# First FFN layer: a PSUM bank filled whole before it is read, 512 columns per read, and a new order of all operations

## Chip, cores and metric

The kernel runs on one core of one Trainium2 chip. The metric is the device time of one execution in microseconds (us). The figure for a kernel is the median of its runs.

## What is computed

Windowed attention, a real-part 2-D Fourier transform, a normalization and a two-layer feed-forward network (FFN), all in fp32. The shapes are q, k, v of (8, 8, 576, 64), which give 4608 tokens of 512 values, and two FFN weights of 512x2048 and 2048x512.

```python
scores = np.where(mask, scale * q @ k.T, -1e9)      # window of 64 positions
attn = softmax(scores) @ v                          # 8 heads of 64
x = attn.transpose(0, 2, 1, 3).reshape(B, S, 512)
u = x + np.real(np.fft.fft(np.fft.fft(x, axis=1), axis=2))
un = (u - mean(u)) / np.sqrt(var(u) + 1e-6)
out = u + np.maximum(un @ w_ch1, 0.0) @ w_ch2
```

## The kernel before

**Tiling.** The 4608 tokens are 36 tiles of 128 tokens. `attn_tile` does the attention of one tile, `fft` the transform of one batch entry, `norm_tile` the sum with the transform and the normalization. Two tiles make a chunk of 256 tokens (`CH`), and there are 18 chunks. fp32 accuracy is reached by splitting every operand into two fp16 parts and multiplying three of the four combinations (`PASSES`), so each logical product is three matmuls. Only the first tiles and the first chunk (chunk 0, the "plain" one) run in true fp32. Chunks 0 to 12 use `ffn(c)`, which the change rewrites; chunks 13 to 17 use `ffn7(c)`, a form of the second layer with seven products instead of eight, whose code the change leaves alone.

**The FFN step.** `ffn(c)` runs over f = 0..15, blocks of 128 of the 2048 hidden values. The first layer of block f (L1405) writes 128x256 fp32, that is half of a PSUM bank: blocks 2p and 2p+1 are the two halves of one bank `ph` (tag `f1`, two banks in all). I call them the first and the second half of pair p. Each half is 12 matmuls of 256 columns. The result is read twice: ScalarE (ACT) applies the ReLU and stores the high fp16 part `hh` (L1420), then VectorE (DVE) stores the low part, max(ph, 0) minus the high part (L1423). I call these two the eviction of a half. They are issued for every half by itself, 256 columns each; there are four `hh` buffers. The second layer of block f (L1386) then takes `hh` as stationary operand: 6 matmuls of 512 columns into the two banks `po`. When all 16 blocks are in, DVE adds `po` to the residual `xu` (L1443) and SyncE stores it.

**Order of the work.** Nothing is left to a scheduler at run time. Every operation is handed to a planner, `Plan.op`, with an engine, an assumed duration, a priority, and the buffers that it reads, writes and holds. `Plan.order` walks the engines in model time and emits all operations in one global order, which becomes each engine's program order. FFN matmuls have priorities from 1e6 up, so TensorE (PE) uses them as filler between attention and transform work; evictions have priority -10, ahead of nearly everything on ACT and DVE. The tables `NUDGE`, `LEAD` and `BIAS` shift priorities and engine choices of single operations. They are numbers found by a search, one set per kernel. Some elementwise operations may go to DVE or to GpSimd (POOL), as the planner finds (`alt`). While the program has not reached the FFN, planned gaps of PE are filled with dummy matmuls (`warm`, L1685). Waits between engines are put in by the framework from the tiles that the emitted operations touch.

Three things in the code matter for what follows. `holds=[bpair]` keeps a bank until both its halves are evicted. In `op("PE", ..., bank1, ..., [bph] if f % 2 else [bph, bfirst], holds=[bpair])` a second half is ordered after the first half and after nothing else. The eviction of the first half may stand in the emitted order ahead of the second half's matmuls or behind them.

```python
"xe": 1, "r3": 3, "fh": 5, "g": 2, "mp": 2, "mt": 1, "un": 2, "up": 1, "big": 4, "hh": 4,
op("PE", 1.73 if plain else 1.31, 1e6 + 32 * c + 2 * f, bank1, [Bu[c], *bws, bfirst], [bph] if f % 2 else [bph, bfirst], holds=[bpair])
op("ACT", 0.28, -10, lambda g=h_part: g(0), [bph], [bh], holds=[bpair])
```

Of the kernel before, what the change touches and what calls it, by code (L numbers as in the profile page):

```python
# [63 lines left out]
    "": {0: 3.6, 1: -0.1, 2: 2.4, 3: -4.7, 4: 0.6, 5: -15.8, 6: -1.7, 7: 0.7, 8: -10.1, 10: 8.4, 11: 17.7},  # L64
    "even": {0: -15.1, 1: 6.7, 2: 27, 3: 18, 4: -20.7, 5: -8.2, 6: -2, 7: 10.7, 8: -16.2, 9: 30.8, 10: -1.9, 11: -5.8, 12: 14.5, 13: -1.2, 14: -0.8, 15: -18.3, 16: 12.5, 18: -0.9, 19: -14.6, 20: -0.5, 22: 7.1, 23: 16.8, 24: -24.7, 25: -1, 26: 19, 27: -1.4, 28: 3.9, 29: -7.5, 30: 1.6, 31: 7.5, 32: -1.3, 34: -9.3, 35: 0.6, 36: -77.6, 37: 16, 38: -6.9, 39: -15.3, 40: -26, 41: 2.8, 43: 10.1, 44: 5},
    "ffn7": {0: 13, 1: -5.4, 2: 0.7, 3: 0.8, 4: 12.9, 5: -11.4, 6: 4.6, 8: 5.2, 9: -4, 10: 0.2, 11: -11.1, 13: -21.7, 14: 2.4, 15: 13, 16: -8.2, 17: 2.1, 18: 6.5, 19: -6.9, 21: 31.5, 22: -9.4, 23: -1.3, 24: 9.8, 25: -3.1, 26: -2.1, 27: 18.5, 28: 34.5, 29: 14.4, 30: 5.9, 31: -10.6, 32: -2.3, 33: 0.3, 34: 5.7, 35: 3, 37: 7.4, 38: 2, 39: 20.6, 40: -4.3, 41: 9.3, 43: -1.2, 44: 1.1, 45: -1.1, 46: 3.9, 47: 19, 48: 0.9, 50: 1.1, 51: 1.4, 52: -1.8, 53: 2.3, 54: -0.5, 55: -26.2, 57: -1.4, 58: 0.2, 59: -23.3, 60: -6.3, 61: -1.3, 62: 3.3, 63: 14.3, 64: -1.6, 65: 7.3, 66: 9.5, 67: 7, 68: 0.6, 69: 4.5, 70: -15.4, 71: -4.1, 72: 2.5, 73: 20.1, 74: 4.1, 75: -9.1, 76: 6.7},
    "first": {0: 9.1, 2: -4.8, 3: -2.3, 4: -2.5, 5: -3.9, 6: 48.2, 7: -4.8, 8: -7.6, 9: -1.3, 12: -12, 13: -1.6, 14: -2.4, 15: 0.4, 16: -1.4, 17: -6.8, 18: -6.5, 19: 3.5, 20: -20.5, 21: -14.9, 22: -5.2, 23: 35.3, 24: 23.3, 25: -13.8, 26: -30.6, 27: 44.4, 28: 0.9, 29: -6.7, 30: 1.2, 32: -0.8, 33: 18, 34: 12, 35: 11.7, 60: -4.6, 61: -1.3, 62: 16.6, 63: -3.1, 70: -19},
    "norm": {0: 9.7, 1: 4.6, 2: -5.6, 3: -5.3, 4: 22.8, 5: -8.4, 6: 0.7, 8: -0.2, 10: 4.1},
    "odd": {0: -6.1, 1: 8.3, 2: -10.5, 3: -0.9, 4: -0.1, 5: 0.4, 6: -10, 7: 12.3, 8: 1, 9: -21.6, 10: 11.6, 11: 11.4, 12: 0.2, 13: 0.5, 14: 0.5, 15: -5.7, 17: -7.6, 18: 2.3, 19: 2.1, 20: 7.5, 21: -3.7, 22: 0.5, 23: -8.9, 24: 1, 25: -1.2, 26: -0.3, 27: 6, 28: 0.8, 29: 8.5, 31: 12.9, 32: -4, 33: -5.6, 35: 8.9, 36: 17.5, 37: 6.6, 38: 4.2, 39: -6.6},
    "part": {1: -2},  # L70
    "piece": {0: 28.4, 2: -6.6, 3: 7, 4: -0.6},
    "prep": {0: -4.8, 1: -0.4, 2: 3.9, 4: 14.6, 5: -3.5, 6: -28.8, 7: 4.1, 8: 6.4, 10: 1.8, 11: -2.4},
    "scale": {0: -15.1, 2: -2.4, 3: -0.8, 4: 5.4},
    "split": {0: -7.5, 1: 4.1, 2: 1, 3: 0.9, 4: -0.5, 6: 24.5, 7: 5.8, 8: -1.2, 9: 3, 10: 32.6, 11: -1.8, 12: -24, 13: 3.6, 14: 0.9, 15: -7.4, 16: -0.2, 17: -1.2, 18: 1.3, 19: 0.8, 20: 2, 22: -22, 23: 14.6, 24: 29.2, 25: 2, 26: -12.3, 28: -29.8, 29: 3.4, 30: -18.6, 31: 16, 32: 2.1, 33: -31.6, 50: 0.3, 51: -2, 53: -20.8, 54: 1.5, 55: -1.9, 56: 7.8, 57: -15.2},
    "tail": {0: -8.3, 1: 3.4, 2: 0.2, 10: 28.5, 11: -0.7, 12: -0.7},
    "whole": {0: 4, 1: 4.2, 2: 3.1, 3: 9.3, 4: -3, 5: 27.2, 6: 15.9, 7: -2.2, 8: 8.6, 9: 14.4, 10: -1.8, 12: 50.7, 13: 4, 14: 15.5, 15: 6.6, 16: 0.5, 17: 2, 18: -0.1, 19: 6.3, 20: 1.7, 21: -1.3, 22: -1.3, 23: -8.4, 50: -16.8, 51: -5.1, 55: 29.8, 56: 1.4, 57: -6.4},
# [124 lines left out]
class Plan:  # L201
# [6 lines left out]
    PATIENT = {"DVE": 0, "ACT": 0.25, "POOL": 0.25, "DMA": 0}  # L208
# [169 lines left out]
def attn_fft_ffn_kernel(ctx: ExitStack, tc: tile.TileContext, q, k, v, w1, w2, gidx, dft_d, dft_s, mask, out):  # L378
# [11 lines left out]
        "xe": 1, "r3": 3, "fh": 5, "g": 2, "mp": 2, "mt": 1, "un": 2, "up": 1, "big": 4, "hh": 4,  # L390
# [978 lines left out]
    def ffn(c):  # L1369
# [7 lines left out]
        def second(f, bh):  # L1377
            def go():
                if f == 0:
                    t["po"] = [bank("f2", f"po{c}_{i}", (P, DM)) for i in range(2)]  # L1380
                hh = t["hh", f]
                for i in range(2):
                    sl = slice(P * i, P * i + P)
                    mm = [(hh[:, sl], wf[1][f])] if plain else [(hh[:, a, sl], wp[1][:, f, b_]) for a, b_ in PASSES]
                    for x, (l_, r_) in enumerate(mm):
                        nc.tensor.matmul(  # L1386
                            t["po"][i], l_, r_, start=(f == 0 and x == 0), stop=(f == NKF - 1 and x == len(mm) - 1)
                        )
# [328 lines left out]
```

## Time and profile before

| | before |
|---|---|
| three runs | 988.84, 991.28, 986.29 us; median 988.84 us |
| profiled execution | 987.79 us, of which the span of the trace is 986.0 us |
| PE, matmuls | 959.6 us busy, 97% of the span, 9362 matmuls |
| DVE | 748.6 us, 76% |
| ACT | 463.4 us, 47% |
| POOL | 186.3 us, 19% |
| granted PE clock, mean | 0.995 of 2.4 GHz |

Each engine is a queue that runs in its program order. An engine's busy time counts instructions, and its idle time counts the gaps before them; a gap's "releaser" is what ended the wait. Matmuls overlap one another, so a group's busy time is the union of their spans, while "mean ns" is the length of one from issue to landing. In a timeline the step from one group's start to the next group's start is the cost on PE.

### The profile page before, as it was taken

Reading aid. Unit: us, or ns where it says so; the run is one execution under the profiler, and the core shown is the slowest. Engines: PE = TensorE matmul, PEld = TensorE weight load, DVE = VectorE, ACT = ScalarE, POOL = GpSimd, SP = SyncE. Lnnn points to the kernel's source line nnn. Section 1 sums busy time; section 2 is a strip of 40 time slices with the busy share of each in tenths; the row PEclk is TensorE's granted clock in tenths of the full one; section 3 lists DMA queues with packets and bytes.
Section 4 is the critical chain, followed back from the end, with each engine's and each line's share of the span. In section 5 each row is a group of like instructions: output and inputs, shape, how many; then the busy total and the mean of one; then the engine's idle time right before and its main releaser. Section 6 shows DMA issues by size and latency. Waiting matters only on the chain.

```text
span 986.0 us, 23773 instructions
## 1 busy us (share of the span) xinstructions
PE 959.6 (97%) x9362; PEld 718.1 (73%) x9362; DVE 748.6 (76%) x1926; ACT 463.4 (47%) x1218; POOL 186.3 (19%) x196
## 2 busy tenths in 40 slices
PE   8999999999999999999999999999989999999997
PEld 6867677666676677666776676667666788888886
DVE  4878988878876887768777786788887986676436
ACT  5756687643553444545553553456322243333312
POOL 2111012122332222312213322221113101100000
PEclk9999999999999999999999999999999999999999
DMA  9988884238999768797858479975423312221000
GB/s 196 272 231 246 244 172 85 86 75 194 159 214 182 172 127 204 151 189 160 185 142 197 109 186 195 185 159 137 87 59 79 60 54 63 66 65 33 1 23 22
DMA packets 316704, 134.76 MB, mean 137 GB/s; under 512 B 293032, under 2 KB 293160, under 8 KB 316592
## 3 DMA queue, kind: packets, MB, share of 16 engines
q1 hardware_dynamic: 313872, 124.33, 56.1%
q0 software_dynamic: 2720, 8.92, 3.6%
q8 instruction: 73, 1.20, 0.5%
q14 instruction: 39, 0.32, 0.1%
HBM read 62.85 MB, written 22.04 MB: 86 GB/s over the span
## 4 chain that ended last, share of the span: by engine, by line
PE 78%; DVE 11%; DMA 5%; SPq 2%; ACT 2%; issue 1%; POOL 0%; DVEq 0%; ACTq 0%; POOLq 0%
PE ph L1405 23%; PE po L1386 20%; PE ph L1527 11%; PE q L1582 9%; PE pa L778 3%; PE pz L1101 2%; PE pg L1049 2%; PE psc L666 2%; DVE hh L1423 2%; DVE y L825 1%; DMA pt<-flex 1%; PE psc L680 1%; DMA kst<-flex 1%; PE pp L724 1%; SPq L744 1%
## 5 line engine op out<-in xcount | busy, mean ns | idle before, releaser
L1405 PE MATMUL ph<-uhl,w0s 128*128 128x256 f16 (+1 forms) x2424 | 311.6, 279 | 10.8 <-DVE hh L1423 9.6
L1386 PE MATMUL po<-w1s,hh 128*128 128x512 f16 (+1 forms) x1216 | 310.8, 391 | 0.0
L1405 PEld LDWEIGHTS <-w0s 128*128 128x128 f16 x2304 | 224.9, 98 | 74.4 <-issue 15.1
L1420 ACT ACTIVATE hh<-ph 128x256 f16<-128x256 f32 x192 | 73.9, 385 | 239.7 <-PE ph L1405 199.7
L1386 PEld LDWEIGHTS <-hh 128*128 128x128 f16 x1152 | 109.8, 98 | 96.2
L1423 DVE SCALAR_TENSOR_TENSOR hh<-ph,hh 128x256 f16<-128x256 f32 x192 | 80.6, 421 | 86.5 <-ACT hh L1420 60.6
L1527 PE MATMUL ph<-uhl,w0s 128*128 128x256 f16 x960 | 108.6, 273 | 0.0
L1527 PEld LDWEIGHTS <-w0s 128*128 128x128 f16 x960 | 93.9, 98 | 11.5
L1210 POOL TENSOR_TENSOR rs<-mv,mhalf 128x1 f32<-128x1 f32 x36 | 22.0, 610 | 279.9 <-DVE mv L1206 278.7
L1546 ACT ACTIVATE flex<-ph 128x512 f32<-128x512 f32 x40 | 23.9, 599 | 98.0 <-PE ph L1527 97.9
L1551 DVE TENSOR_TENSOR flex<-flex 128x256 f32<-128x256 f32 x80 | 34.6, 432 | 35.9 <-ACT flex L1546 34.1
L709 ACT ACTIVATE pr<-pr,nm 128x128 f32<-128x128 f32 x184 | 58.3, 394 | 3.5 <-DVE nm L700 3.5
L1582 PEld LDWEIGHTS <-qbd 128*128 128x128 f16 x480 | 47.0, 98 | 5.4
L738 POOL TENSOR_TENSOR flex<-pr,flex 128x512 f16<-128x512 f32 x24 | 29.4, 1227 | 96.0 <-ACT flex L485 47.0
L1186 POOL DMA_INDIRECT mt<-md,gix x34 | 36.6, 1077 | 45.9 <-DMA md<-mp 36.9
L793 ACT ACTIVATE xa<-pa,rc 128x64 f32<-128x64 f32 x184 | 41.5, 324 | 7.7 <-DVE rc L786 3.6
L700 DVE CUSTOM_DVE_ANT_0 pr<-psc,mskb 128x128 f32<-128x128 f32 x184 | 41.3, 285 | 4.1 <-PE psc L666 3.9
L1582 PEld LDWEIGHTS <-kst 128*128 128x128 f16 x360 | 35.2, 98 | 4.1
L778 PE MATMUL pa<-v,pt 128*64 128x65 f16 (+1 forms) x1328 | 31.0, 201 | 1.2 <-DMA pt<-flex 1.2
L576 POOL TENSOR_TENSOR flex<-qn,flex 128x1024 f16<-128x1024 f32 x11 | 23.7, 2153 | 43.3 <-ACT flex L485 26.2
L825 DVE TENSOR_TENSOR y<-xa 128x256 f32<-128x256 f32 x60 | 29.2, 528 | 0.9 <-ACT xa L793 0.7
L1582 PE MATMUL q<-w1s,qbd 128*128 128x256 f16 x240 | 29.5, 273 | 0.0
(219 smaller groups left out, 1520.6 us busy)
## 6 DMA issues: line engine op xcount, KB each, us to landing
wd<-in_moe_w_ch SPq DMA_DIRECT2D x26, 512.0 KB
out<-xu SPq DMA_DIRECT2D x36, 256.0 KB
kn<-in_k SPq DMA_DIRECT2D x32, 256.0 KB
qn<-in_q SPq DMA_DIRECT2D x32, 256.0 KB
xd<-xa SPq DMA_DIRECT2D x30, 256.0 KB
xu<-xd SPq DMA_DIRECT2D x30, 256.0 KB
flex<-in_v SPq DMA_DIRECT2D x20, 256.0 KB
v<-v SPq DMA_DIRECT2D x36, 130.0 KB
```

Of the source, the lines that this page charges most:

```text
L700: nc.vector.tensor_tensor_reduce(out=t["pr", jj][:, hp], in0=t["ps", jj][:, hp], in1=mskb[:, m : m + P], scale=-0.125, scalar=3.0e38, op0= ...
L709: nc.scalar.activation(pr, src, AF.Exp, bias=t["nm", jj][:, hp : hp + 1], scale=-1.0)
L778: nc.tensor.matmul(pa[half_, hh], pt, v_, start=(x == 0), stop=(x == len(mm) - 1))
L793: nc.scalar.mul(xv[:, hh], pa[:, hh, 0:64], rc[:, hh])
L825: eng.tensor_tensor(out=o, in0=p0, in1=p1, op=al)
L1186: nc.gpsimd.indirect_dma_start(out=mts[T], out_offset=None, in_=mds[pb][0 : HR if n < 4 else 2 * HR], in_offset=bass.IndirectOffsetOnAxis( ...
L1386: nc.tensor.matmul(t["po"][i], l_, r_, start=(f == 0 and x == 0), stop=(f == NKF - 1 and x == len(mm) - 1))
L1405: nc.tensor.matmul(ph, l_, r_, start=(x == 0), stop=(x == len(mm) - 1))
L1420: nc.scalar.activation(t["hh", f][:, 0], ph, AF.Relu)
L1423: nc.vector.scalar_tensor_tensor(out=hh[:, 1], in0=ph, scalar=0.0, in1=hh[:, 0], op0=ALU.max, op1=ALU.subtract)
L1527: nc.tensor.matmul(ph, l_, r_, start=(x == 0), stop=(x == len(mm) - 1))
L1582: nc.tensor.matmul(t["q"][q_][:, y], l_[:, a, i, m], r_(b_, m), start=(s_ + y + m + x == 0), stop=(s_ == 3 and m == 1 and x == 2 and (y == ...
```

## The change

The two halves of a pair are computed into their bank as before, and only then is the bank read: one ACT instruction and one DVE instruction of 512 columns per pair, in place of two and two of 256. `hh` becomes one tile for both blocks of a pair, with two buffers in place of four (the same bytes). The bank belongs to the pair as a whole, so `holds` is gone. The second layer's priorities go by pairs. `PATIENT["POOL"]` goes from 0.25 to 1 (how far the planner lets POOL wait for an operation of better priority). All three tables are searched anew: `NUDGE` (17 lines), `LEAD` and `BIAS`, of which one line stands here. Line numbers behind L1405 shift by one or two. In the built order, ahead of the first FFN matmul there stand 55 dummy matmuls and the scores of nine tiles (before: 46 and eight). `u_lo` (L1233) goes from 24 on DVE and 10 on POOL to 31 and 3, `k_lo` (L565) from 10 and 13 to 15 and 8. The matmuls that do real work are the same ones, as many as before.

```diff
-    "part": {1: -2},
+    "part": {0: 1.1, 1: -5.2},
...
-    PATIENT = {"DVE": 0, "ACT": 0.25, "POOL": 0.25, "DMA": 0}
+    PATIENT = {"DVE": 0, "ACT": 0.25, "POOL": 1, "DMA": 0}
...
-        ... "big": 4, "hh": 4,
+        ... "big": 4, "hh": 2,
...
-            op("PE", 1.73 if plain else 1.3, 1e6 + 32 * c + 2 * max(f, 1) + 5, go, [bh, Bw[1][f + at]], bpo)
-        for f in range(NKF):
-            bph, bh = Buf(), Buf("hh")
-            if f % 2 == 0:
-                bpair, bfirst = Buf("f1"), Buf()
+            op("PE", 1.73 if plain else 1.3, 1e6 + 32 * c + 4 * (f // 2) + 7 + 0.5 * (f % 2), go, [bh, Bw[1][f + at]], bpo)
+        for pr in range(NKF // 2):
+            bph, bh, bfirst = Buf("f1"), Buf("hh"), Buf()
+            for f in (2 * pr, 2 * pr + 1):
...
+                op("PE", 1.73 if plain else 1.31, 1e6 + 32 * c + 2 * f, bank1, [Bu[c], *bws, *([bfirst] if f % 2 else [])], [bph] if f % 2 else [bph, bfirst])
...
-                    t["hh", f] = sb([P, 2, CH], F16, "hh", f"hh{c}_{f}")
-                    nc.scalar.activation(t["hh", f][:, 0], ph, AF.Relu)
+                    t["hh", pr] = sb([P, 2, 2, CH], F16, "hh", f"hh{c}_{pr}")
+                    nc.scalar.activation(t["hh", pr][:, 0], ph, AF.Relu)
...
-            op("PE", 1.73 if plain else 1.31, 1e6 + 32 * c + 2 * f, bank1, [Bu[c], *bws, bfirst], [bph] if f % 2 else [bph, bfirst], holds=[bpair])
-            op("ACT", 0.28, -10, lambda g=h_part: g(0), [bph], [bh], holds=[bpair])
+            op("ACT", 0.5, -10, lambda g=h_part: g(0), [bph], [bh])
             if not plain:
-                op("DVE", 0.33, -10, lambda g=h_part: g(1), [bph], [bh], holds=[bpair], port=False)
+                op("DVE", 0.56, -10, lambda g=h_part: g(1), [bph], [bh], port=False)
```

**Place 1: the second half of a pair, on PE.** This is pair 3 of chunk 9 (the same pair of the same chunk in both). `hh` is the second layer's stationary operand, `w0s` the first layer's weights, `uhl` the normalized chunk; what an instruction waits for stands in brackets by engine. Before:

```order
L1386 LDWEIGHTS hh_4_9038
L1386 MATMUL po_1_8925<-w1s,hh_4_9038 128x512
L1405 LDWEIGHTS w0s
L1405 MATMUL ph_6_9072<-uhl_7924,w0s 128x256 [waits DVE_49]
L1405 LDWEIGHTS w0s
L1405 MATMUL ph_6_9072<-uhl_7924,w0s 128x256
```

With the change:

```order
L1386 LDWEIGHTS hh_1_8687
L1386 MATMUL po_1_8711<-w1s,hh_1_8687 128x512
L1406 LDWEIGHTS w0s
L1406 MATMUL ph_3_8807<-uhl_7778,w0s 128x256
L1406 LDWEIGHTS w0s
L1406 MATMUL ph_3_8807<-uhl_7778,w0s 128x256
```

The wait for DVE ahead of the second half is gone. Before, 56 of the 96 second halves of chunks 1 to 12 wait for DVE and 18 more for ACT; with the change none does.

**Place 2: the evictions of that pair, on DVE.** `ph_6` (before) and `ph_3` (with the change) are the bank. Before:

```order
L489 CAST flex<-kn_8922 128x8x64 [waits DMAHW7_49]
L565 TENSOR_TENSOR flex<-kn_8922,flex 128x8x64 [waits DVE_49]
L1423 SCALAR_TENSOR_TENSOR hh_6_9094<-ph_6_9072,hh_6_9094 128x256 [waits Activation_49]
L855 TENSOR_TENSOR yT_8544<-py_9057 128x4x128 [waits DMAHW0_49]
L1198 TENSOR_TENSOR xu_8937<-xu_8937,mt_9068 64x511 [waits DMAHW3_49,DMASW4_49]
L1199 TENSOR_TENSOR xu_8937<-xu_8937,mt_9068 64x1
L1201 TENSOR_TENSOR xu_8937<-xu_8937,mt_9068 64x512
L1203 BN_STATS st_9116<-xu_8937 128x6 [waits DVE_49]
L1205 BN_AGGR mv_9118<-st_9116 128x2 [waits DVE_49]
L1206 TENSOR_SCALAR mv_9118<-mv_9118 128x1 [waits DVE_49]
L1423 SCALAR_TENSOR_TENSOR hh_7_9127<-ph_6_9072,hh_7_9127 128x256 [waits Activation_49]
```

With the change:

```order
L738 TENSOR_TENSOR flex<-pr_0_8690,flex 128x4x128
L489 CAST flex<-kn_8412 128x8x64 [waits DMAHW6_49,DMAHW1_49]
L1421 SCALAR_TENSOR_TENSOR hh_2_8804<-ph_2_8721,hh_2_8804 128x512 [waits Activation_49]
L1421 SCALAR_TENSOR_TENSOR hh_3_8854<-ph_3_8807,hh_3_8854 128x512 [waits Activation_49]
L1198 TENSOR_TENSOR xu_8740<-xu_8740,mt_8856 64x511 [waits DMAHW7_49,DMAHW2_49,DMASW4_49]
L1199 TENSOR_TENSOR xu_8740<-xu_8740,mt_8856 64x1
```

One eviction of 512 columns stands where two of 256 stood, and it can still stand right behind an instruction that waits for a transfer (DMAHW).

**Place 3: the first use of the evicted pair, on PE.** The end of pair 4's second half and the start of pair 3's second layer, same chunk, with the change (before, the second layer of a block began with the same two kinds of wait):

```order
L1406 MATMUL ph_4_8860<-uhl_7778,w0s 128x256
L1386 LDWEIGHTS hh_3_8854 [waits Activation_49]
L1386 MATMUL po_0_8710<-w1s,hh_3_8854 128x512
L1386 LDWEIGHTS hh_3_8854
L1386 MATMUL po_0_8710<-w1s,hh_3_8854 128x512
L1386 LDWEIGHTS hh_3_8854 [waits DVE_49]
L1386 MATMUL po_0_8710<-w1s,hh_3_8854 128x512
```

The second layer is now the first on PE to wait for an eviction. Between the end of a pair's second half and this place stand four groups of PE work or more (half, second layer, half, second layer), with a few exceptions near two.

## Rows read from the trace of the kernel before

**Rows 1.** The page: span, busy time by engine.
```profile
span 986.0 us, 23773 instructions
PE 959.6 (97%) x9362; PEld 718.1 (73%) x9362; DVE 748.6 (76%) x1926; ACT 463.4 (47%) x1218; POOL 186.3 (19%) x196
```

**Rows 2.** Waits of PE: engine, line, releaser, total us, times, longest us.
```profile
PE ph L1405 <- DVE hh L1423: 9.6, 10, 2.0
...
PE pk L550 <- DMA kn<-in_k: 1.9, 1, 1.9
PE pa L778 <- DMA pt<-flex: 1.2, 2, 0.9
...
PE ph L1405 <- ACT hh L1420: 0.5, 1, 0.5
```

**Rows 3.** Busy time by stretch: us and instructions of each engine, then PE clock.
```profile
0.00:25.00 25.00, 21.56 (x283) 16.26 (x284) 10.64 (x24) 13.37 (x43) 5.01 (x19) 1.00 0.97 197
25.00:50.00 25.00, 24.20 (x310) 21.36 (x311) 21.15 (x47) 19.35 (x64) 2.71 (x2) 1.00 0.93 274
50.00:75.00 25.00, 22.58 (x184) 16.97 (x183) 19.62 (x49) 12.90 (x42) 3.47 (x5) 0.93 0.84 223
75.00:100.00 25.00, 24.07 (x235) 17.59 (x233) 22.34 (x51) 18.59 (x56) 2.58 (x3) 1.00 0.86 256
200.00:700.00 500.00, 491.86 (x5038) 343.93 (x5036) 388.11 (x1153) 233.12 (x647) 128.24 (x120) 1.00 0.78 165
787.00:960.00 173.00, 173.00 (x1584) 154.90 (x1583) 112.12 (x213) 56.42 (x81) 10.54 (x12) 1.00 0.16 43
960.00:986.00 26.00, 20.86 (x192) 18.46 (x189) 16.53 (x30) 7.51 (x10) 0.00 (x0) 0.95 0.06 21
```

**Rows 4.** Timeline around 594 us (place 1): start, us, engine, line, operation [idle before].
```profile
590.29 1.47 PE L1405 MATMUL ph<-uhl,w0s 128*128 128x256 f16 x12
591.60 1.46 PE L1386 MATMUL po<-w1s,hh 128*128 128x512 f16 x6
...
592.90 1.47 PE L1405 MATMUL ph<-uhl,w0s 128*128 128x256 f16 x12
594.21 1.46 PE L1386 MATMUL po<-w1s,hh 128*128 128x512 f16 x6
594.47 0.39 ACT L1420 ACTIVATE hh<-ph 128x256 f16<-128x256 f32 x1 [1.75 <-PE ph L1405]
595.21 0.43 DVE L489 CAST flex<-kn 128x512 f16<-128x512 f32 x1 [2.04 <-DMA kst<-flex]
595.67 0.69 DVE L565 TENSOR_TENSOR flex<-kn,flex 128x512 f16<-128x512 f32 x1
596.28 0.42 DVE L1423 SCALAR_TENSOR_TENSOR hh<-ph,hh 128x256 f16<-128x256 f32 x1
596.75 1.47 PE L1405 MATMUL ph<-uhl,w0s 128*128 128x256 f16 x12 [1.08 <-DVE hh L1423]
```

**Rows 5.** Timeline around 735 us, the longest of these waits.
```profile
733.56 2.56 POOL L953 TENSOR_TENSOR xe<-yT 128x1156 f32<-128x1156 f32 x1 [13.69 <-ACT yT L485]
733.87 2.81 DVE L1482 TENSOR_TENSOR sw<-sw,w1s 128x512 f32<-128x512 f32 x1
736.60 0.41 DVE L1423 SCALAR_TENSOR_TENSOR hh<-ph,hh 128x256 f16<-128x256 f32 x1
...
737.06 3.15 PE L1405 MATMUL ph<-uhl,w0s 128*128 128x256 f16 x17 [2.04 <-DVE hh L1423]
```

**Rows 6.** Busy time by stretch behind the two waits of about 2 us.
```profile
55.20:58.50 3.30, 3.30 (x19) 3.11 (x18) 2.99 (x8) 0.81 (x2) 0.56 (x1) 0.50 0.87 187
737.80:741.20 3.40, 3.40 (x18) 2.35 (x17) 2.87 (x6) 0.00 (x0) 0.00 (x0) 0.50 0.58 171
741.30:744.70 3.40, 3.40 (x27) 2.53 (x26) 1.90 (x6) 1.63 (x6) 0.93 (x1) 1.00 0.36 137
```

**Rows 7.** Groups by line: count, busy us, mean ns, idle before and its releasers.
```profile
L1423 DVE SCALAR_TENSOR_TENSOR hh<-ph,hh 128x256 f16<-128x256 f32 x192 | 80.6, 421 | 86.5 <-ACT hh L1420 60.6 <-PE ph L1405 25.1
L1420 ACT ACTIVATE hh<-ph 128x256 f16<-128x256 f32 x192 | 73.9, 385 | 239.7 <-PE ph L1405 199.7 <-DVE hh L1423 27.5 <-PE po L1386 9.9
L1546 ACT ACTIVATE flex<-ph 128x512 f32<-128x512 f32 x40 | 23.9, 599 | 98.0 <-PE ph L1527 97.9
L1059 DVE SCALAR_TENSOR_TENSOR g<-pg,g 97x512 f16<-97x512 f32 x21 | 14.4, 684 | 2.2 <-ACT g L485 2.0
```

**Rows 8.** Groups by line: work that can go to DVE or POOL.
```profile
L1233 DVE TENSOR_TENSOR up<-un,up 128x512 f16<-128x512 f32 x24 | 18.9, 788 | 2.1 <-ACT up L485 1.6
L1233 POOL TENSOR_TENSOR up<-un,up 128x512 f16<-128x512 f32 x10 | 12.6, 1262 | 33.6 <-DVE rc L783 19.2 <-ACT up L485 8.3 <-DVE up L489 5.3
L565 DVE TENSOR_TENSOR flex<-kn,flex 128x512 f16<-128x512 f32 x10 | 7.7, 768 | 0.2
```

**Rows 9.** Groups by line: the dummy matmuls, and the fp16 score matmuls.
```profile
L1685 PE MATMUL warm<-ident 128*128 128x256 f16 x46 | 9.2, 343 | 2.0 <-POOL ident masks.py:199 2.0
L666 PE MATMUL psc<-kst,qbd 128*64 128x128 f16 x736 | 27.2, 221 | 0.2 <-DMA qbd<-flex 0.2
```

More of the change, by code (lines that the diff above doesn't have):

```diff
@@ L70 @@
-    "part": {1: -2},
[L71 to L74, printed above, removed]
@@ L77 @@
+    "tail": {0: -17.8, 1: 3.2, 2: 7.5, 10: 4.8, 11: -2.4, 12: -10.8},
+    "whole": {0: 0.9, 1: 1.8, 2: 8.9, 3: 6.6, 4: 14.2, 5: 14, 6: -7.8, 7: -12.5, 8: -4.6, 9: 25.4, 10: -12, 11: -5.7, 12: 56.9, 13: 3.3, 14: 35.6, 15: 3.8, 16: 9.2, 17: -0.1, 18: 0.7, 20: 0.3, 21: -3.6, 22: -0.2, 23: -13.6, 50: -34.3, 55: 29.7, 56: -1.4, 57: 0.8},
 }
@@ L1380, in go @@
                     t["po"] = [bank("f2", f"po{c}_{i}", (P, DM)) for i in range(2)]
-                hh = t["hh", f]
+                hh = t["hh", f // 2]
                 for i in range(2):
                     sl = slice(P * i, P * i + P)
-                    mm = [(hh[:, sl], wf[1][f])] if plain else [(hh[:, a, sl], wp[1][:, f, b_]) for a, b_ in PASSES]
+                    mm = [(hh[:, f % 2, sl], wf[1][f])] if plain else [(hh[:, a, f % 2, sl], wp[1][:, f, b_]) for a, b_ in PASSES]
                     for x, (l_, r_) in enumerate(mm):
@@ new lines, in second, with bank1, h_part @@
+            op("PE", 1.73 if plain else 1.3, 1e6 + 32 * c + 4 * (f // 2) + 7 + 0.5 * (f % 2), go, [bh, Bw[1][f + at]], bpo)
+        for pr in range(NKF // 2):
+            bph, bh, bfirst = Buf("f1"), Buf("hh"), Buf()
+            for f in (2 * pr, 2 * pr + 1):
+                g0, c0 = 4 * (f // 4), (f % 4) * P
+                def bank1(f=f, pr=pr, g0=g0, c0=c0):
+                    if f % 2 == 0:
+                        t["ph", pr] = bank("f1", f"ph{c}_{pr}", (P, 2, CH))
+                    ph, u = t["ph", pr][:, f % 2], uhls[c]
+                    if plain:
+                        mm = [(wf[0][g0 + kc][:, c0 : c0 + P], u[:, kc]) for kc in range(4)]
+                    else:
+                        mm = [(wp[0][:, g0 + kc, a, c0 : c0 + P], u[:, b_, kc]) for kc in range(4) for a, b_ in PASSES]
+                    for x, (l_, r_) in enumerate(mm):
+                        nc.tensor.matmul(ph, l_, r_, start=(x == 0), stop=(x == len(mm) - 1))
+                bws = [Bw[0][g0 + kc + at] for kc in range(4)]
+                op("PE", 1.73 if plain else 1.31, 1e6 + 32 * c + 2 * f, bank1, [Bu[c], *bws, *([bfirst] if f % 2 else [])], [bph] if f % 2 else [bph, bfirst])
+            def h_part(z, pr=pr):
+                ph = t["ph", pr]
+                if plain:
+                    t["hh", pr] = sb([P, 2, CH], F32, "hh", f"hh{c}_{pr}")
+                    nc.scalar.activation(t["hh", pr], ph, AF.Relu)
+                elif z == 0:
+                    t["hh", pr] = sb([P, 2, 2, CH], F16, "hh", f"hh{c}_{pr}")
+                    nc.scalar.activation(t["hh", pr][:, 0], ph, AF.Relu)
+                else:
+                    hh = t["hh", pr]
@@ L1425, in h_part @@
                     )
-            bws = [Bw[0][g0 + kc + at] for kc in range(4)]
-            op("PE", 1.73 if plain else 1.31, 1e6 + 32 * c + 2 * f, bank1, [Bu[c], *bws, bfirst], [bph] if f % 2 else [bph, bfirst], holds=[bpair])
-            op("ACT", 0.28, -10, lambda g=h_part: g(0), [bph], [bh], holds=[bpair])
+            op("ACT", 0.5, -10, lambda g=h_part: g(0), [bph], [bh])
             if not plain:
-                op("DVE", 0.33, -10, lambda g=h_part: g(1), [bph], [bh], holds=[bpair], port=False)
+                op("DVE", 0.56, -10, lambda g=h_part: g(1), [bph], [bh], port=False)
             if prev:
-                second(*prev)
-            prev = (f, bh)
-        second(*prev)
+                for f in (0, 1):
+                    second(2 * (pr - 1) + f, prev)
+            prev = bh
+        for f in (0, 1):
+            second(NKF - 2 + f, prev)
         for i in range(2):
```

84 lines of the change are left out of this document (33 added, 51 removed).

## Prediction

> **What bounds the kernel now.** I read the page first [rows 1]: TensorE has matmuls in flight for 959.6 of 986.0 us, no other engine is over 76%, and the change takes no matmul of real work away. So the question is only what PE loses. The stretches [rows 3] show where. From 787 to 960 us PE is full (173.00 of 173); that is the part of chunks 13 to 17, which the change only reorders. In the first 100 us PE misses 3.44 + 0.80 + 2.42 + 0.93 = 7.6 us, while DMA is 84 to 97% busy; 9.2 us more are dummy matmuls that fill planned gaps [rows 9]. At the end (960 to 986) 5.1 us are missing, the last sums and the store. From 200 to 700 it is 8.1 us. All of PE's idle time is 986.0 - 959.6 = 26.4 us, 2.7%; less the end and the first 2.0 us [rows 9], no reordering can give more than about 20 us.
>
> The list of PE's waits [rows 2] then names one large item: `ph` for DVE's eviction, 9.6 us in 10 waits, and once 0.5 us for ACT's. Everything else is at most 1.9 us.
>
> The timeline shows what kind of wait it is [rows 4]. A first half runs from 592.90, a second-layer group from 594.21; the second half of the same bank could start at 594.21 + 1.30 = 595.51. It starts at 596.75, just behind the DVE eviction (596.28) **of the first half of its own bank**. That eviction stood in DVE's queue behind a cast which waited 2.04 us for a transfer to land. Place 1 of the change shows the same wait in the program. The step costs 596.75 - 595.51 = 1.24 us, 0.16 us more than the idle time printed, because matmul groups otherwise overlap by 0.16 (1.47 long, 1.31 apart). I went through the other ten in the same way: all eleven are second halves that wait for the eviction of their own first half. In the longest one [rows 5] DVE was held by a 2.81 us addition that overlaps a POOL addition of 2.56 us.
>
> The reason is room. Behind a first half stands one second-layer group, so its eviction must be done 1.30 - 0.16 = 1.14 us after its end. ACT starts 0.10 us after the half (594.37 to 594.47), takes 0.39, DVE 0.42: 0.93 us with the handover. The room is 0.2 us, and anything that makes DVE late shows on PE.
>
> **The change part by part.**
>
> *The wait of second halves goes.* 11 waits, 9.6 + 0.5 us idle, and 11 x 0.16 us of lost overlap: 11.9 us [rows 2, 4]. In the built order no second half waits for an eviction any more.
>
> *A stretch at half clock goes.* Right behind the longest wait (2.04 us) the granted clock is 0.50 from 737.8 to 741.2, that is 1.2 in place of 2.4 GHz: 18 matmuls, against 27 in the next 3.4 us [rows 6]. The same stands from 55.2 to 58.5, where PE had waited 1.9 us for `kn` [rows 2]; behind the shorter waits between 200 and 700 the clock stays at 1.00 [rows 3]. Half of 3.4 us is 1.7 us. It goes with its wait.
>
> *Fewer, longer evictions.* DVE: 192 x 421 ns = 80.8 us become 96 x 684 ns = 65.7, by the nearest row of 512 columns out of PSUM (L1059). ACT: 192 x 385 = 73.9 become 96 x 599 = 57.5 (L1546) [rows 7]. Both engines get about 15 us free, but neither bounds anything by its sum, so I count nothing. DVE gets back most of it: 7 + 5 low parts come over from POOL, 12 x 0.78 = 9.4 us [rows 8].
>
> *New first waiter: the second layer* (place 3). A pair's eviction now takes 0.10 + 0.60 + 0.02 + 0.68 = 1.40 us from the end of the pair. In regular order four groups stand between, 2 x (1.31 + 1.30) - 0.16 = 5.06 us: room 3.7 us in place of 0.2. The next write into the bank comes one group later still. The lateness seen before was at most 2.04 + 0.16 + 0.2 = 2.4 us, so regular places should take it. But at eight of the 96 pairs the built order leaves only two groups, 2.45 us, room 1.05, and at two more about 0.7 us beyond that. Queued behind such a wait are the rest of the second layer and everything else on PE. Bounds: 0 us, if DVE is nowhere late there; 10 x (2.4 - 1.05) = 13.5 us if it is late by the worst case each time. Before, one second half in five of the 56 with such a wait was late. I take 4 us, nearer the lower end for that reason, and above it because the searched order uses the new room: at place 2 two pairs' evictions stand together behind a cast that waits for a transfer.
>
> *Start-up.* Nine more dummies at 0.2 us [rows 9] mean that the planner sees some 2 us more of gaps before the FFN starts; one tile more of attention stands ahead of it, which only changes places with filler. I take +2 us. Bounds: -3 us (some of the 7.6 us idle closes, and the 1.7 us of slow clock behind the wait for `kn`) to +6 us (a tile's chain is not covered).
>
> *The rest of the order.* Other waits between 100 and 787 us come to 26.4 - 7.6 - 5.1 - 10.1 = 3.6 us. New orders of 24,000 instructions will close some and open others: 0, within -3.5 to +3.5.
>
> Sum against the profiled execution: 987.8 - 11.9 - 1.7 + 4 + 2 = **980.2 us**. The median of the runs is 1.05 us above that execution, so the forecast is 981.3, rounded 981, 0.8% less than 988.84. A measurement of this kernel can tell about 0.5%, 4.9 us, from no change.
>
> A row and a rule on the work that comes over to DVE. The low part of k takes DVE 768 ns in the mean and 0.69 us where nothing stands against it [rows 4, 8]: 0.08 us lost on each, and 1 us on the twelve. The Trainium skill (SBUF — State Buffer, Who interferes with whom) says that a DVE instruction with two SBUF inputs is fully blocked while a GpSimd instruction that reads SBUF holds the shared port pair; a DVE instruction with one SBUF input, as the eviction, is not blocked, though it queues behind one that is. By that rule twelve more DVE instructions can each be held for a POOL instruction's 1.26 us, 15 us of lateness spread over the FFN, and the new waits would go to their upper end, 991, which is the first rival below. The trace bears the block out in rows 5, and as a mean far less.
>
> **The rivals.**
>
> *The gain is handed back at the second layer.* The order was searched for a model in which transfers land on time and POOL and DVE never overlap; given 3.7 us of room, the search fills it with other DVE work, and the same late casts stop `po` in place of `ph`. For it: place 2, and DVE at 78% between 200 and 700 us [rows 3]. Against it: half as many evictions, and only ten narrow places. It decides once most of those ten are late by 2.4 us: new waits 13.5 in place of 4, 981.3 + 9.5 = 991, no change.
>
> *Slower: waits of 2 us with a slow clock behind them.* A DVE instruction held for 2.8 us or by a landing, ahead of a pair's eviction, stops PE for 2 us, and each such wait costs 2.0 + 0.16 + 1.7 = 3.9 us, since the clock falls behind it [rows 5, 6]. For it: before, one wait in eleven reached that size, and a pair's eviction stops two groups of second layer at once. Against it: with 1.05 us of room the lateness must be over 3 us, with 3.7 over 5.7, and none was seen. From five such waits on (19.5 us in place of 4) the time is 981.3 + 15.5 = 997, 0.8% slower.
>
> *The new wait on PE itself.* In the built order the first matmul of 74 pairs waits for PE's own semaphore. If each drained the array, 74 x 0.16 = 12 us [rows 4]: 993. Against it: what it waits for stands 36 matmuls or more earlier in the built program, and the score matmuls, many with such a wait already, show 0.2 us of idle time in 736 [rows 9].
>
> **How the numbers follow.** Forecast 0.70; handed back 0.15; slower 0.13; PE's own wait 0.02. Within the forecast the unknown terms (new waits 0 to 8, start-up -3 to +6, rest -3.5 to +3.5) give 973 to 988; below 983.9 I put 0.56 of the 0.70, the other 0.14 is within 0.5%. So faster 0.56, same 0.14 + 0.15 + 0.02 = 0.31, slower 0.13. The range 973 to 992 takes in the forecast and the handing back and leaves out the slower case and a little below.
>
> **What would show it.** Right: PE's wait list has no `ph` for DVE or ACT beyond 1 us, `po` (L1386, until now 0.0) shows a few us, no window between 200 and 780 us has a clock of 0.50, DVE has 96 evictions near 0.68 us and ACT 96 near 0.60. PE's idle time falls from 26.4 to about 21 us, the dummies take 11 us. Wrong: `po` waiting more than 10 us in total, two or more half-clock stretches, or PE missing over 12 us in the first 100 us.

## The result, and the profile after

The changed kernel takes 979.84 us in the median against 988.84 us before. The ratio is 0.9907 with an interval of 0.9887 to 0.9927: faster by 0.9%, where 0.8% and 981 us were forecast. The profiled execution went from 987.79 to 977.76 us. One of the 13 executions of the changed kernel took 2532.78 us; the ratio leaves it out, and without it the median is 979.0 us.

The page's first lines answer to [rows 1].

```profile
span 976.0 us, 23525 instructions
PE 956.7 (98%) x9371; PEld 718.0 (74%) x9371; DVE 741.5 (76%) x1833; ACT 452.1 (46%) x1125; POOL 180.3 (18%) x185
```

PE lost 2.9 us of busy time, and its idle time fell from 26.4 to 976.0 - 956.7 = 19.3 us. The list of PE's waits answers to [rows 2] (engine, line, releaser, total us, times, longest us):

```profile
PE pa L778 <- DVE w0s L1293: 3.3, 1, 3.3
PE pa L778 <- DMA pt<-flex: 2.3, 3, 1.1
PE warm L1683 <- POOL mhalf L444: 1.3, 1, 1.3
PE psc L666 <- DMA qbd<-flex: 1.3, 1, 1.3
```

No row of the whole list is left for `ph` or for `po`. In a second trace of the same kernel (span 976.5 us; its repeated run is under Experiments) there is one:

```profile
PE ph L1406 <- DVE hh L1421: 0.9, 1, 0.9
```

In the built order this is a first half, which waits until the pair that last stood in its bank is evicted, and not a second half. The groups by line (count, busy us, mean ns, idle before) are those of the first profile again, and answer to [rows 7 to 9]:

```profile
L1406 PE MATMUL ph<-uhl,w0s 128*128 128x256 f16 x2304 | 281.5, 273 | 0.0
L1386 PE MATMUL po<-w1s,hh 128*128 128x512 f16 x1152 | 280.3, 379 | 0.0
L1421 DVE SCALAR_TENSOR_TENSOR hh<-ph,hh 128x512 f16<-128x512 f32 x96 | 66.0, 687 | 61.6 <-ACT hh L1418 61.2
L1418 ACT ACTIVATE hh<-ph 128x512 f16<-128x512 f32 x96 | 57.3, 597 | 168.0 <-PE ph L1406 154.8 <-PE po L1386 12.9
L1683 PE MATMUL warm<-ident 128*128 128x256 f16 x55 | 10.3, 327 | 1.3 <-POOL mhalf L444 1.3
L1233 DVE TENSOR_TENSOR up<-un,up 128x512 f16<-128x512 f32 x31 | 21.3, 686 | 2.6 <-ACT up L485 2.4
```

Busy time by stretch (PE, PEld, DVE, ACT, POOL, then PE clock, DMA share, GB/s) answers to [rows 3]:

```profile
0.00:25.00 25.00, 22.71 (x290) 17.22 (x291) 12.53 (x30) 11.97 (x35) 2.75 (x15) 1.00 0.90 179
25.00:50.00 25.00, 21.11 (x279) 18.50 (x278) 18.03 (x41) 14.73 (x50) 1.80 (x2) 0.93 0.95 257
50.00:75.00 25.00, 23.51 (x204) 17.81 (x203) 21.98 (x53) 15.55 (x54) 2.82 (x5) 1.00 0.89 221
75.00:100.00 25.00, 22.90 (x231) 17.09 (x230) 21.80 (x56) 15.73 (x48) 3.53 (x5) 1.00 0.79 221
200.00:700.00 500.00, 496.03 (x5089) 347.86 (x5088) 389.28 (x1083) 230.38 (x592) 127.84 (x117) 1.00 0.83 166
700.00:777.00 77.00, 77.00 (x688) 55.87 (x687) 59.82 (x119) 24.61 (x59) 18.10 (x16) 1.00 0.30 77
960.00:976.00 16.00, 10.46 (x96) 9.12 (x94) 7.16 (x14) 1.78 (x2) 0.00 (x0) 0.91 0.09 33
```

From 200 to 700 us PE now misses 4.0 us in place of 8.1, and from 700 to 777 nothing. In the first 100 us it misses 2.29 + 3.89 + 1.49 + 2.10 = 9.8 us, 2.2 more than before. At the end it is 5.5 in place of 5.1. The clock stays at 1.00 in the whole middle; the one stretch at half clock before the end lies behind the 3.3 us wait, in the window from 25 to 50.

How near the new first waiter comes to waiting is seen where a pair's eviction ends closest to its reader (timeline: start, us, engine, line, operation):

```profile
725.81 0.68 DVE L1490 TENSOR_TENSOR wt<-sw,wt 128x512 f16<-128x512 f32 x1
726.53 0.69 DVE L1473 TENSOR_TENSOR sw<-w1s 128x512 f32<-128x512 f16 x1
726.80 0.60 ACT L1418 ACTIVATE hh<-ph 128x512 f16<-128x512 f32 x1 [1.46 <-PE ph L1406]
...
728.03 2.94 POOL L953 TENSOR_TENSOR xe<-yT 128x1156 f32<-128x1156 f32 x1 [5.52 <-ACT yT L485]
728.59 1.40 DVE L1441 SCALAR_TENSOR_TENSOR xu<-po,osc,xu 128x512 f32<-128x512 f32 x2
729.91 0.68 DVE L1421 SCALAR_TENSOR_TENSOR hh<-ph,hh 128x512 f16<-128x512 f32 x1
730.51 1.02 DVE L1490 TENSOR_TENSOR v<-sw,v 128x512 f16<-128x512 f32 x1
730.90 1.46 PE L1386 MATMUL po<-w1s,hh 128*128 128x512 f16 x6
```

ACT is done at 727.40, but DVE gets to the eviction at 729.91 and ends at 730.59. The second layer reads it at 730.90: 0.31 us to spare, the least of all 96 pairs. The next is 0.81, and the median 3.8 us.

### The profile page after: what moved, and what is told of

Its sections match the earlier page's. It is cut to its first block, busy times and chain, and to the rows that moved or that the text cites. A ratio compares the mean times of both kernels' runs of the same rounds, so it can differ in the third digit from the quotient of the medians.

```text
span 976.0 us, 23525 instructions
## 1 busy us (share of the span) xinstructions
PE 956.7 (98%) x9371; PEld 718.0 (74%) x9371; DVE 741.5 (76%) x1833; ACT 452.1 (46%) x1125; POOL 180.3 (18%) x185
## 4 chain that ended last, share of the span: by engine, by line
PE 87%; DMA 5%; DVE 3%; SPq 2%; ACT 1%; issue 1%; POOL 0%; DVEq 0%; ACTq 0%; POOLq 0%
PE ph L1406 26%; PE po L1386 25%; PE ph L1525 11%; PE q L1580 9%; PE pa L778 3%; PE pz L1101 2%; PE pg L1049 2%; PE psc L666 2%; DMA qbd<-flex 1%; DMA wd<-in_moe_w_ch 1%; PE psc L680 1%; DMA pt<-flex 1%; PE pp L724 1%; SPq L512 1%; PE pm L1145 1%
## 5 line engine op out<-in xcount | busy, mean ns | idle before, releaser
L1386 PE MATMUL po<-w1s,hh 128*128 128x512 f16 (+1 forms) x1216 | 310.8, 391 | 0.0
L1406 PE MATMUL ph<-uhl,w0s 128*128 128x256 f16 (+1 forms) x2424 | 309.8, 278 | 0.0
L1406 PEld LDWEIGHTS <-w0s 128*128 128x128 f16 x2304 | 223.4, 98 | 60.2 <-issue 0.6
L1386 PEld LDWEIGHTS <-hh 128*128 128x128 f16 x1152 | 110.0, 98 | 96.1
L1418 ACT ACTIVATE hh<-ph 128x512 f16<-128x512 f32 x96 | 57.3, 597 | 168.0 <-PE ph L1406 154.8
L1421 DVE SCALAR_TENSOR_TENSOR hh<-ph,hh 128x512 f16<-128x512 f32 x96 | 66.0, 687 | 61.6 <-ACT hh L1418 61.2
L1210 POOL TENSOR_TENSOR rs<-mv,mhalf 128x1 f32<-128x1 f32 x36 | 24.9, 692 | 280.9 <-DVE mv L1206 244.9
L1549 DVE TENSOR_TENSOR flex<-flex 128x256 f32<-128x256 f32 x80 | 34.3, 429 | 27.8 <-ACT flex L1544 26.4
L793 ACT ACTIVATE xa<-pa,rc 128x64 f32<-128x64 f32 x196 | 43.6, 323 | 14.8 <-DVE rc L786 6.3
L1549 DVE TENSOR_TENSOR kst<-flex,kst 128x768 f16<-128x768 f32 x20 | 19.1, 955 | 18.4 <-ACT kst L1558 18.3
L825 DVE TENSOR_TENSOR y<-xa 128x256 f32<-128x256 f32 x60 | 26.5, 483 | 5.0 <-PE py L895 3.0
```

Source lines behind the costliest of these rows:

```text
L793: nc.scalar.mul(xv[:, hh], pa[:, hh, 0:64], rc[:, hh])
L1386: nc.tensor.matmul(t["po"][i], l_, r_, start=(f == 0 and x == 0), stop=(f == NKF - 1 and x == len(mm) - 1))
L1418: nc.scalar.activation(t["hh", pr][:, 0], ph, AF.Relu)
L1421: nc.vector.scalar_tensor_tensor(out=hh[:, 1], in0=ph, scalar=0.0, in1=hh[:, 0], op0=ALU.max, op1=ALU.subtract)
L1549: return lambda: nc.vector.tensor_tensor(out=o, in0=a, in1=b, op=al)
```

## Experiments

My theory: the gain is the wait of second halves for their own bank's eviction, and nothing else of size. First rival: the newly searched order is the gain. Second rival: fewer and longer evictions relieve DVE and ACT. All times are medians beside runs of the kernel before on the same chip (988.0 to 989.2 us).

**Pairing alone, old order.**

```diff
 (the changed kernel)
-NUDGE, LEAD, BIAS of the changed kernel; PATIENT POOL 1
+those of the kernel before, but "norm" of the changed one and no "prep"; PATIENT POOL 0.25
```

> The changed kernel's pairing (bank filled whole, one 512-column read by each engine, two hh buffers), with the order numbers of the kernel before in all groups but two (norm from the changed kernel, prep empty, since the old ones give no order that fits two hh buffers) and the old PATIENT of POOL. If the removed own-half waits are the gain (my theory), no matmul of line 1406 waits on DVE or ACT by more than 1 us in all, PE's idle time falls by the 9 to 12 us of those waits, and the time is 973 to 983 us, since the rest of the order may cost or give 3.5. If the gain comes from the newly searched numbers, this run stays at 986 to 991 us.

980.81 us, ratio 0.9923 (0.9896 to 0.995). The code starts 55 lines earlier here (L1351 is L1406, L1331 is L1386). Waits of PE:

```profile
PE pk L495 <- DMA kn<-in_k: 3.8, 1, 3.8
PE pa L723 <- DMA pt<-flex: 3.8, 2, 3.1
...
PE po L1331 <- DVE hh L1366: 1.1, 2, 1.0
PE ph L1351 <- DVE hh L1366: 1.1, 1, 1.1
```

The waits on evictions fall from 10.1 to 2.2 us with the old numbers too. The one on `ph` is 0.1 us over the 1 us that I had allowed; in the built order it is a first half that waits for its bank, so no second half waits for its own bank's eviction. What I had expected of PE's idle time did not come in the profiled execution: 982.4 - 956.5 = 25.9 us, only 0.5 less than before, and not 9 to 12 less. Other waits came up in place of the evictions, most of them for transfers: 3.8 us each for `kn` and `pt`, where it was 1.9 and 1.2 [rows 2]. That execution (984.21 us) is 3.4 us above the median of its kernel, and its other executions have no trace. So it is the time that says that the pairing brings the gain: the median is 7.2 us below the kernel before, and the 1 to 2 us to the changed kernel cannot be told from none, since the two intervals overlap. The one trace shows the waits gone, but not PE's idle time with them. Two groups of numbers (`norm`, `prep`) were not the old ones.

**New order alone.**

```diff
 (the kernel before)
-NUDGE, LEAD, BIAS, PATIENT of the kernel before
+NUDGE, LEAD, BIAS, PATIENT of the changed kernel
```

> The kernel before with every order number of the changed kernel and its PATIENT of POOL; the eviction still follows each block of 128 columns. My theory: the second block still waits for the eviction of the first, so lines 1405 keep 7 to 14 us of waits on DVE and ACT, and the time is 984 to 994 us. If the searched order is the gain, 978 to 982 us.

1025.34 us, ratio 1.0379 (1.0351 to 1.0408): the rival is out, but my own range missed too. Waits of PE, then the busy time by stretch around the longest:

```profile
PE ph L1405 <- DVE hh L1423: 12.4, 11, 4.0
PE pa L778 <- DMA pt<-flex: 11.6, 4, 7.3
PE pa L778 <- DMA v<-v: 5.0, 2, 3.0
```

```profile
331.00:351.00 20.00, 10.04 (x156) 7.80 (x157) 13.55 (x43) 8.93 (x29) 5.83 (x6) 0.50 0.75 169
```

The own-half waits are there as expected (12.4 us for DVE, 0.4 for ACT, all of them second halves in the built order). What I had not priced is that the numbers put PE's work ahead of transfers in places that fit only the other code: 7.3 us for one `pt`, and then 20 us at a clock of 0.50, in which PE is busy for 10.0.

**Filled whole, read in two pieces.**

```diff
-nc.scalar.activation(t["hh", pr][:, 0], ph, AF.Relu)
+for y in range(2):
+    nc.scalar.activation(t["hh", pr][:, 0, y], ph[:, y], AF.Relu)
...
+for y in range(2):   # the DVE eviction in the same way
```

> The changed kernel in its own order, with each 512-column eviction split again into two 256-column instructions on ACT and on DVE, both behind the filled bank. Twice about 0.42 us on DVE for 0.687 us: DVE gets 96 x 0.15 = 15 us more work, and each pair's hh is ready about 0.15 us later, against a least lead of 0.30 us and a median of 3.8 us from eviction to first reader in the changed kernel. My theory (the wait, not the number of instructions, is the gain): 978 to 982 us, no wait on hh above 0.1 us. If the shorter work of DVE and ACT is the gain, it is given back: 985 to 990 us.

981.37 us, ratio 0.9916 (0.9887 to 0.9946), the same as the changed kernel. The group by line:

```profile
L1423 DVE SCALAR_TENSOR_TENSOR hh<-ph,hh 128x256 f16<-128x256 f32 x192 | 72.1, 417 | 54.8 <-ACT hh L1419 53.9
```

Two short evictions back to back cost 0.75 us together, not 0.84, so DVE's evictions rise from 66.0 to 72.1 us and its whole busy time by 9.4, not by 15. None of it shows in the time. The waits on `hh` were not below 0.1 us, as I had expected: one of 0.4 us at `po`, and one of 1.0 us at a first half that waits for its bank, of the size of the 0.9 us in the changed kernel's second profile. The length of the instructions is not the gain; the moment of reading is.

**The wait put back.**

```diff
 (in bank1, ahead of the second half's matmuls)
+elif pr < 2 or ("used", f - 5) in t:      # a half buffer is free
+    h_half(0, 0, pr), plain or h_half(1, 0, pr)
...
-"hh" in two buffers of 2 x 256 columns, read once per pair
+"hh" in four buffers of 256 columns; h_part evicts what is left of the pair
```

> The changed kernel with its own order of PE and its own numbers, but the first block of a bank is read again (256 columns, ACT then DVE) ahead of the second block's matmuls, wherever one of the four half buffers is free by then: 103 of the 144 second blocks wait for that eviction again; the others keep the changed kernel's order. Nothing else of the order moves on PE. The distance between the two blocks is 6 matmuls of the second layer (6 x 0.39 = 2.35 us) in 56 pairs, as in 59 pairs of the kernel before. My theory: PE waits at line 1408 and its copies come back at the size of before, 7 to 15 us in some 8 to 20 waits, DVE gets 96 x 2 short evictions again, and the time is 985 to 995 us. If the searched order alone were the gain, 978 to 982 us.

1025.43 us, ratio 1.0374 (1.0351 to 1.0397), 46 us above the changed kernel; I had expected 5 to 15. One wait explains it:

```profile
PE ph L1422 <- DVE hh L1402: 40.3, 43, 3.4
```

The timeline shows how:

```profile
252.25 1.46 PE L1386 MATMUL po<-w1s,hh 128*128 128x512 f16 x6
...
252.51 0.38 ACT L1399 ACTIVATE hh<-ph 128x256 f16<-128x256 f32 x1
253.64 1.08 PE L666 MATMUL psc<-kst,qbd 128*64 128x128 f16 x32
254.32 0.29 DVE L700 CUSTOM_DVE_ANT_0 pr<-psc,mskb 128x128 f32<-128x128 f32 x1 [1.33 <-PE psc L666]
...
255.17 0.42 DVE L1402 SCALAR_TENSOR_TENSOR hh<-ph,hh 128x256 f16<-128x256 f32 x1
255.64 1.47 PE L1422 MATMUL ph<-uhl,w0s 128*128 128x256 f16 x12 [0.92 <-DVE hh L1402]
```

ACT reads the half 0.1 us after it is done, but on DVE the eviction stands behind maxima that wait for the scores (`psc`). In this run 91 of the 96 second halves start within 0.3 us of the end of that eviction. In the kernel before it was 42, and 37 others started ahead of it, because its planner had emitted the second half first. In the built order all 96 second halves of chunks 1 to 12 wait for DVE here, where before 56 did and 18 for ACT; the run puts back more than was taken away. So the waits of 10.1 us were what was left after the planner had worked around the dependency; an order that does not know of it pays 41 us. My expectation also erred in the distance: six matmuls of the second layer take 1.13 us from the end of one half to the start of the next, as the prediction's room of 1.14 had it, not 6 x 0.39.

**Evictions late: three times, then twice.**

```diff
-nc.vector.scalar_tensor_tensor(out=hh[:, 1], in0=ph, ...)
+for y in range(3):   # 2 in the other run; the same values are written each time
+    nc.vector.scalar_tensor_tensor(out=hh[:, 1], in0=ph, ...)
```

> The changed kernel in its own order, with the DVE eviction of each pair issued three times, so hh is ready 2 x 0.687 = 1.37 us later. From the leads of the changed kernel's trace (0.30, 0.81, 8 of 1.02 to 1.09, 1.24 us, the other 85 above 1.37) the second layer's first reader would now wait 11 times, 4.4 us in all, if an exposed new wait costs its own length: 982 to 986 us. DVE's busy time rises by 132 us to some 873. If the new wait is worth less than that because something else then ends sooner, 979 to 981 us; if DVE becomes the bound or other work behind the evictions is late, above 988 us.

> The changed kernel with the DVE eviction of each pair issued twice: hh is 0.69 us later, DVE has 66 us more work (741 to some 807 us). Issued three times it cost 44 us, where the leads from eviction to first reader alone gave 4.4. By the leads alone only the pair with 0.30 us of lead waits, 0.4 us: 979 to 981 us. If what counts is the work queued behind the evictions on DVE (y, g, xu, which also had to wait with three), the cost starts at the first addition and is about half of 44 us or somewhat less: 990 to 1003 us. I hold the second likelier.

1023.47 us (ratio 1.036, 1.0333 to 1.0388) and 990.56 us (1.0016, 0.9997 to 1.0034), that is 44 and 11 us above the changed kernel. Waits of PE with three, and then with two:

```profile
PE po L1386 <- DVE hh L1422: 10.9, 10, 2.1
PE py L895 <- DVE y L825: 7.8, 7, 1.4
...
PE pz L1101 <- DVE g L1059: 3.5, 5, 1.3
...
PE po L1386 <- DVE xu L1442: 2.6, 4, 1.0
```

```profile
PE pa L778 <- DMA pt<-flex: 5.1, 5, 2.0
...
PE psc L666 <- DMA qbd<-flex: 2.7, 2, 2.2
PE po L1386 <- DVE hh L1422: 1.7, 2, 1.4
```

With three, the forecast by leads was 11 waits on `hh` and 4.4 us; it came to 10 waits and 10.9 us. The evictions also start later: 0.75 us behind the end of ACT's in the median, where in the changed kernel it is 0.03. A lead is not a cushion that each eviction has for itself. By the list of waits, PE waits for DVE for 30.7 us in all, with 3.7 in the changed kernel; 12.3 of them are for evictions, and the other 18 for other work of the same engine. With two, `hh` stops `po` for only 1.7 us; the rest lies in small waits, many for transfers. Whether these are late because the DVE work that feeds them is late was not tried apart. DVE's busy time rose by 9, 58 and 122 us (split, twice, three times; 66 and 132 were forecast for the last two), and the price was 1.5 (not distinguishable from none), 11 and 44 us.

**No dummies at the start.**

```diff
-for _ in range(int((gap - WARM[1]) / 0.21)):
+for _ in range(int((gap - WARM[1]) / 0.21) if gap > 1e9 else 0):
```

> The changed kernel without any of its 55 warming matmuls in the start (10.3 us of PE's busy time), all else in its order. They were put where PE would be idle, so at full clock their time turns into idle time and the sum stays: 977 to 983 us. If they keep the granted clock up, half-clock stretches beyond the one of 3.4 us appear in the first 90 us, each worth up to 1.7 us: 980 to 986 us. If they delay work that is ready, it falls to 974 to 977 us.

979.54 us, ratio 0.9902 (0.9882 to 0.9922). The 55 dummies neither cost nor bring anything that can be measured. The execution that was profiled is the slowest of the seven (989.34 us, the others 976.70 to 979.97), so its trace is not typical. In it PE is idle for 16.1 us of the first 100, where it was 9.8 with 10.3 us of dummies, and the half clock comes there once, as in the changed kernel (37.8 to 41.2 us).

**The start's longest wait.** First two weight loads go behind the copy of `v`; then the DVE conversions go behind the maxima as well.

```diff
 (order of the emitted operations, nothing else)
-... load w0 4, load w0 2, copy v, load v ...
+... copy v, load v, load w0 4, load w0 2 ...
 (second run, DVE)
-... convert w0 4, w0 2, next piece ... nm x4
+... nm x4 ... convert w0 4, w0 2, next piece
```

> The changed kernel with two of the three weight loads that SP issues at 25.0 us (w0 pieces 4 and 2, 512 KB each) and their first DVE conversions moved behind the next copy of v and the v load, nothing else. The 3.3 us wait of pa at 37.6 us ended just as that copy of v could land (issued at 29.9 us, 7.6 us to landing in the row on v loads of that stretch, behind four 512 KB loads). If the copy of v is what PE waited for, the wait falls below 1 us, the half-clock stretch behind it (3.4 us, so 1.7 us lost) goes too, and the time falls by up to 5 us: 975 to 978 us, less if the loads that now come later hold DVE and PE up at 40 to 92 us (the first 100 us move much data: share 0.84 to 0.97 in the kernel before); then 978 to 981 us. If DVE's conversion was the releaser, the wait stays at 3 us.

> As the run before with v ahead of the loads, and besides the first two DVE conversions of the three weight pieces (w0 4, w0 2 and the one behind them) stand behind the softmax maxima nm that PE's next work hangs on. In that run DVE waited 1.66 us for a weight load at 38.07 us with nm queued behind it, and PE then 3.6 us for pr. If in-order queueing behind the weight loads is what makes the start-up waits, both go and the half-clock stretch behind them too: PE's idle time in the first 100 us falls from 9.8 by 4 to 6 us, and the time is 973 to 977 us. If the loads themselves set the start (DMA share 0.79 to 0.95 in its four stretches), another wait comes later in the first 100 us: 977 to 981 us.

> The changed kernel itself, unaltered, on the same chip as the run above and beside the same runs of the kernel before: 978 to 982 us, so that the two can be compared directly.

979.35, 979.50, and 979.42 us for the changed kernel again (0.9911, 0.9909 and 0.992). PE's longest wait between 30 and 55 us, in the first run and in the second:

```profile
PE py L891 <- ACT pr L709: 3.6, 1, 3.6
```

```profile
PE pa L778 <- DVE pt L489: 4.0, 1, 4.0
```

The 3.3 us wait goes when the copy of `v` is ahead. The conversion which the list names was moved in the same run, so this alone does not tell the two apart; in the repeated run of the changed kernel the list names the copy itself (2.7 us), which makes the copy the likelier one. But a wait of the same size comes up 4 us later, and with that one out of the way another at 48 us. Idle time in the first 100 us stays at 8.9 and 10.1 us, beside 9.8 and 10.6 in the two profiles of the changed kernel. The DMA share there is 0.79 to 1.00. That the loads set the start fits all four profiles; it was not shown by making the loads smaller, so it stays open. No variant is faster than the changed kernel by more than the medians scatter.

## Why the prediction was right, and where its sizes were off

- *The wait of second halves*, -11.9: the size is borne out, the reading in ten of the eleven waits. 10.1 us of idle time are gone from the list, and PE's busy time fell by 2.9, in which the lost overlap (1.8) and the half clock (1.7) go out and the dummies (1.1) come in, -2.4 by these three. With the old order the pairing still removes 7.9 of the 10.1, and the wait put back costs the gain and more. But the longest wait, 2.04 us, is no second half [rows 5]. Its surroundings in the kernel before:

```profile
730.50 1.47 PE L1405 MATMUL ph<-uhl,w0s 128*128 128x256 f16 x12
732.54 0.39 ACT L1420 ACTIVATE hh<-ph 128x256 f16<-128x256 f32 x1 [2.18 <-DVE hh L1423]
733.54 1.47 PE L1405 MATMUL ph<-uhl,w0s 128*128 128x256 f16 x12
...
737.23 0.38 ACT L1420 ACTIVATE hh<-ph 128x256 f16<-128x256 f32 x1
```

  The half computed from 733.54 on is read by ACT only at 737.23, after PE has gone on at 737.06; so PE cannot have waited for that. The DVE eviction that it waited for (736.60) is of the half from 730.50, the second one of an earlier pair, and in the built order PE goes on with a first half that takes over that pair's bank. The change keeps this dependency. So 8.1 us of idle time were second halves at their own bank, and 2.0 us of idle time, 0.16 of overlap and the 1.7 us of half clock behind it hung on another wait. It is 0.0 in the one profile of the changed kernel and 0.9 us in the other. Why it shrank, by the room that a pair has or by the new order, was not tried apart.
- *The stretch at half clock*, -1.7: borne out in the middle; no window from 100 to 960 us is below 1.00. It went with the wait for a bank just described, not with a second half's.
- *Fewer, longer evictions*, 0: borne out. 687 and 597 ns stand against 684 and 599 forecast, and splitting them again costs nothing measurable.
- *New first waiter*, +4: mis-sized; it measured 0.0. The step took the worst lateness of before, 2.4 us, against a room of 1.05 us at the narrow places. In the trace DVE gets to the eviction 0.03 us behind ACT at each of the eight narrowest places; at three places with more room it is 2.5 to 3.9 us late, more than the 2.4 that was taken as the worst. That the two did not meet was luck in part: in the second profile of the same kernel one narrow place is 1.35 us late. Its caution was not groundless: with 0.31 us left at one place and DVE loaded further, exactly this wait comes (10.9 us).
- *Start-up*, +2: mis-sized; 2.2 us more idle and 1.1 us more of dummies, 3.3 in all, within its bounds of -3 to +6. The term was sized by the nine new dummies alone. They fill gaps and do not make them: without any the time is the same, and in the one trace of that run 6.3 us of their 10.3 are idle time in the first 100 us.
- *The rest*, 0: waits in the middle other than own-half went from 3.6 to 4.0 us, the end from 5.1 to 5.5.

By the measured terms: -11.9 - 1.7 + 2.2 + 1.1 + 0.4 + 0.4 = -9.5 of the 10.0 us between the two profiled executions. The 2.4 us by which the profiled execution lies under the forecast 980.2 are the `po` term, less what start, middle and end took. Terms of a few us are not safe here: PE's idle time is 19.3 us in one profile of the changed kernel and 22.1 in the other. The prediction's range of 973 to 988 is also narrower than the sum of the bounds that it names (981.3 - 12.5 = 968.8 to 981.3 + 11.5 = 992.8), and it gives no reason for that.

Of the rivals, *handed back* and *slower* needed `po` waits, and there are none. *PE's own semaphore* would show as idle time at L1406 or as more busy time; the idle time there is 0.0, and PE's busy time fell. On the rule on DVE beside POOL that the prediction weighed: in the timeline above, DVE's eviction (0.68) and the sums from PSUM (1.40 for two) run at their usual length beside POOL's 2.94 us, while L1490, two SBUF inputs, takes 1.02 us; a like one took 0.68 at 725.81, and POOL ended at 730.97. That agrees with the Trainium skill (SBUF — State Buffer, Who interferes with whom) on which of the two is held. The price of 15 us that I worked out from it did not come: the 31 low parts on DVE average 686 ns, against 788 before [rows 8].

## What to carry to other kernels

Where one bank is filled in pieces and read in between, the read becomes a condition of the next write; look in the list of waits for a tile that waits for its own eviction, and fill the bank whole if its reader is several groups away. The list does not say which half waits: follow the reads in the timeline, since a half that waits for its own bank's first half and one that waits for a bank to come free look the same there. A searched order belongs to the code that it was searched for: on the old code the new numbers cost 37 us, on the new code the old ones (but for two groups) cost nothing measurable. The idle time that a dependency shows is what the order could not hide, not what the dependency would cost in another order (10 against 41 us here).

## What I had not expected of the hardware

The half clock did not follow from a wait's length alone in these traces. Waits of 1.9 and 2.0 us had a stretch of 3.4 us at half clock behind them [rows 6]; the 2.7 us wait at 37 us in the repeated run of the changed kernel had none, and neither had one of 3.5 us at the same place in the run with three evictions; in both the clock was 1.00 from 25 to 50 us. Around the waits of 3.6 and 4.0 us in the two runs on the start the clock was at 0.50 for 6.8 us each. Busy time by stretch, first and second of these runs:

```profile
40.50:47.20 6.70, 5.28 (x24) 5.28 (x25) 5.81 (x11) 4.46 (x16) 0.08 (x1) 0.50 1.03 316
```

```profile
46.10:52.80 6.70, 4.79 (x43) 4.17 (x44) 5.97 (x12) 1.85 (x8) 2.87 (x3) 0.50 0.85 289
```

Both stretches begin while PE still waits (it starts again at 41.92 and 48.01 us). What decides it was not tried.
